# FNet mixing with a gated SwiGLU on one core: a written issue order for gate/up, and the later stages' preparation in three pieces

## The chip, the core and the metric

The kernel runs on one core of a Trainium2 chip. A core has a matrix engine (PE, with PEld as its weight loads), a vector engine (DVE), a scalar engine (ACT), a general engine (POOL, which here mostly issues DMAs) and a sync engine (SP, which here only issues DMAs). Each engine takes its own instructions in the order of its program and waits, at the head of that order, until what the instruction needs is there. The metric is device time in microseconds (us) of one execution; before the change it was 740.35 us (median of three runs, 739.05 to 740.51).

## What is computed

```python
def reference(A_x, A_dft_seq_re, A_dft_seq_im, A_dft_hid_re, A_dft_hid_im,
              B_x, B_w1, B_w3, B_w2, gate_w):
    x = A_x                                             # 1 x 2048 x 512, float32
    g = sigmoid((x * gate_w).sum(-1, keepdims=True))
    a = einsum("bsd,ed->bse", x, A_dft_hid_re)
    b = einsum("bsd,ed->bse", x, A_dft_hid_im)
    y = einsum("ts,bse->bte", A_dft_seq_re, a) - einsum("ts,bse->bte", A_dft_seq_im, b)
    h = silu(einsum("bsd,df->bsf", x, B_w1)) * einsum("bsd,df->bsf", x, B_w3)   # f = 1376
    out = einsum("bsf,fd->bsd", h, B_w2)
    return g * y + (1 - g) * out
```

## The kernel before

**Arithmetic.** Every float32 operand of a matrix product is split into a rounded high part and the remaining low part (`split`, lines 109 to 111: ACT copies the high part out, DVE subtracts it from the source to get the low part). A product is three matmuls: high by high, high by low, low by high (`mm3`, line 113). On top of that, 2x2 block products are done with seven block products in place of eight, from sums and differences of the blocks ("forms").

**Stages.** The first stage is gate/up: 22 items, each one pair of gate and up weight blocks (`c`, 128 columns of `w1` and of `w3`) with one half of the tokens (`g`). Items 0 to 8 are `c` 0 to 8 with `g` 0, items 9 to 12 are `c` 9 and 10 with both halves, items 13 to 21 are `c` 0 to 8 with `g` 1. Item 0 is done plainly; the others go through `gate_up(n)` in a loop over `n`. After them come the main stages: steps (`step(m)`) of 12 matmuls that multiply the sequence DFT blocks (`cc`), then the stored results of gate/up (`hsp`), then intermediate results (`zsp`) with stationary forms of `x`, `w2` and the hidden DFT.

**An item.** It has seven products of six matmuls each. Two of them, "first" products, belong to item `n + 3` (`first1`, `first2`, LOOK = 3), five to item `n`. In PE's order: product 4 of item `n` into bank X (from `wb`), product 5 into bank Z (`wb`), first product of item `n + 3` (`wa`), product 3 into X (`wb`), product 2 into Z (`wa`), the second product of item `n + 3` into bank Y (`wa`), and product 6 into X (`wb`). Between them ACT and DVE read the banks: u2 copies X (line 292), u4 copies Z (line 294), s1 copies the first product (line 249), `u4 += X` (line 297), `u2 += Z` (line 299), `u2 *= s1` (line 300), `s1 += Y` (line 257) and its silu (line 259), the silu of X (line 304) and `g1 *= u4` (line 305). POOL then stores h (line 283). A product that adds into a bank must wait for the copy that reads it first: product 3 for u2, product 2 for u4, product 6 for `u4 += X`. The bank of the first product of item `n + 3` is the one that the silu of line 304 of item `n - 1` reads last.

**Weights.** `wa` (three forms) is split from the loaded `ws`; `wb` (four forms) needs four DVE sums of 256 columns (lines 224 to 227) and a split. `wb` of `c` 0 to 8 is stored (line 232) and loaded back (line 209) for the second half of the tokens.

**Work for later stages** is woven into the items through a dictionary `extra`, run at the end of an item: the second half of `x` for gate/up (`xo_sum`, `split_xo`, items 3 to 9), four blocks of `w2` (`prep_w2`, items 9 to 12, stored to `w2sp` by POOL at lines 450 and 452) and seven of the eight stationary forms of `x` (`make_a`, items 13 to 19). A block is loaded at the end of the item before. `w2` works in four wide tiles (`wide`, pool f4_a) and two tiles for the parts (`parts`, pool zo_a); each `prep_w2` takes both of the latter, so that the next one's ACT copies wait for the stores of the last.

**Order.** In the loop over the items only PE's and SP's orders are as written (`manual_schedule` with these two engines, line 566); those of ACT, DVE and POOL are laid out by the framework's planner from its own estimates when the program is built. From line 575 on all engines go as written. After the loop the pools of gate/up are closed and their memory is given to those of the main stages: the buffers of `cc` blocks from 4 on lie over `wb` and `wa`, the tiles of `load_a2` (line 592) over the second half of `x`.

Of the kernel before, what the change touches and what calls it, by code (L numbers as in the profile page):

```python
# [26 lines left out]
K = 9  # L27
XO_AT = 3
W2_AT = (9, 10, 11, 12)
A1_AT = (13, 14, 15, 16, 17, 18, 19)  # L30


@with_exitstack
def fnet_swiglu_gate_kernel(
# [63 lines left out]
    def wide(name):  # L98
        return take(F4, [P, 1024], F32, name)
# [4 lines left out]
    def free(*tiles):  # L104
        for t in tiles:
            _, places, at = HELD.pop(id(t))
            places.append(at)

    def split(hi, lo, src):
        nc.scalar.activation(hi, src, AF.Copy)  # L110
        nc.vector.tensor_sub(lo, src, hi.bitcast(F32))  # L111

# [31 lines left out]
    def splits1(m, t1):  # L144
        split(flat(t1[:, 0, 1:4]), flat(t1[:, 1, 1:4]), m[:, :768])

    def forms1(r, m, t1):
        sums1(r, m, t1)
        splits1(m, t1)

# [24 lines left out]
    def flat_x(ap):  # L175
        return ap.rearrange("p q n -> p (q n)")
# [11 lines left out]
    def sum_xo(g, k, t):  # L188
        ST[g, k] = t
        nc.vector.tensor_sub(t, *(ST[g, v] for v in SUMS[k]))  # L190

    def split_xo(g, k):
        o = XO[g][:, :, OPS.index(k)]
        split(flat_x(o[:, 0]), flat_x(o[:, 1]), ST[g, k])

    WS, WA, WB = {}, {}, {}

    def back(w):
        return w >= NC and SETS[w] > 0
# [7 lines left out]
    def load_wb(w):  # L207
        WB[w] = wbp.tile([P, 2, 4, 256], F32R, tag="wb", name=f"wb{w}")
        nc.sync.dma_start(WB[w].bitcast(F32), wbsp[SETS[w]])

    def prep_wa(w, lo=0, hi=3):

        if lo == 0:
            WA[w] = wap.tile([P, 2, 3, 256], F32R, tag="wa", name=f"wa{w}")
        t = WA[w]
        split(t[:, 0, lo:hi].rearrange("p a n -> p (a n)"),
              t[:, 1, lo:hi].rearrange("p a n -> p (a n)"),
              WS[w][:, lo:hi].rearrange("p a n -> p (a n)"))

    def prep_wb(w):  # L220

        r = WS.pop(w)
        u = wup.tile([P, 4, 256], F32, tag="wu", name=f"wu{w}")
# [3 lines left out]
        nc.vector.tensor_sub(u[:, 3], r[:, 1], u[:, 1])  # L227
        t = WB[w] = wbp.tile([P, 2, 4, 256], F32R, tag="wb", name=f"wb{w}")
        split(t[:, 0].rearrange("p a n -> p (a n)"), t[:, 1].rearrange("p a n -> p (a n)"),
              u.rearrange("p a n -> p (a n)"))  # L230
        if w < K:
            nc.gpsimd.dma_start(wbsp[w], t.bitcast(F32))

# [29 lines left out]
    def put_score(n, j, gate):  # L263


        c, g = ITEMS[n]
        if c < NC - 1:
            return
        if j == 0:
            SC[g] = wide(f"sc{g}")  # L270
        t = SC[g].rearrange("p (b n) -> p b n", b=2)
        nc.scalar.activation(t[F % P :, j], gate[F % P :], AF.Copy)
        if j == 1:
            nc.gpsimd.dma_start(gs[2 * g : 2 * g + 2].rearrange("b o n -> o b n"),
                                t[F % P : F % P + 1])
            extra.setdefault(n + 1, []).append(lambda: free(SC[g]))

# [6 lines left out]

    def second(n, between):
# [6 lines left out]
        nc.scalar.activation(u2, x, AF.Copy)  # L292
# [6 lines left out]
        nc.vector.tensor_add(u2, u2, z)  # L299
        nc.vector.tensor_mul(u2, s1, u2)  # L300
        between[1]()
        prod(x, n, 6, 2, False, True)
        put_score(n, 1, x)
        nc.scalar.activation(g1, x, AF.Silu)  # L304
        nc.vector.tensor_mul(g1, g1, u4)
        store_h(n, h)

    extra = {}

    def gate_up(n):  # L310
        last = NI - 1

        def b0():
            w = WSET[min(n + LOOK, last)] + 1
            if w < len(SETS) and w not in WA and w not in WS:
                load_w(w, 0, 3 if back(w) else 4)
            if n < last and WSET[n + 1] not in WB:
                prep_wb(WSET[n + 1])
            if n + LOOK <= last:
                first1(n + LOOK)  # L320

        def b1():
            if n + LOOK < last and WSET[n + LOOK + 1] not in WA:
                prep_wa(WSET[n + LOOK + 1])
            if n + LOOK <= last:
                first2(n + LOOK)

        if n < last and WSET[n + 1] not in WB and back(WSET[n + 1]):
            load_wb(WSET[n + 1])
        if n + LOOK <= last and WSET[n + LOOK] not in WA:  # L330
            prep_wa(WSET[n + LOOK])
        second(n, (b0, b1))
        for f in extra.get(n, ()):
            f()

# [90 lines left out]
    WS.pop(0)  # L426
    load_w(4)


    def xo_sum(k, b):  # L430
        return lambda: (sum_xo(1, k, ST[1, b]), split_xo(1, k))

    extra[XO_AT - 2] = [lambda k=k: load_xo(1, k) for k in ("B11", "B21", "B12", "B22")]
    for n, f in enumerate((lambda: split_xo(1, "B11"), lambda: split_xo(1, "B21"),
                           xo_sum("T1", "B11"), xo_sum("T2", "B11"), xo_sum("T3", "B12"),
                           xo_sum("T4", "B21"), lambda: split_xo(1, "B22"))):
        extra[XO_AT + n] = [f]
    for n, k in enumerate((("B12",), ("B11", "B21"), ("B22",))):
        extra[XO_AT + 4 + n].append(lambda k=k: free(*(ST[1, b] for b in k)))

    W2R = {}

    def load_w2(p):
        W2R[p] = wide(f"w2r{p}")
        nc.sync.dma_start(W2R[p], w2[p])

    def prep_w2(p):
        r, m, t1, t2 = W2R.pop(p), wide(f"w2m{p}"), parts(f"w2a{p}"), parts(f"w2b{p}")
        forms1(r, m, t1)
        nc.gpsimd.dma_start(w2sp[0][p], t1.bitcast(F32))  # L450
        forms2(r, t2[:, :, :3])
        nc.gpsimd.dma_start(w2sp[1][p], t2[:, :, :3].bitcast(F32))
        free(r, m, t1, t2)

# [5 lines left out]

    def make_a(p, pl=None):
        A1.append((pl or a1).tile([P, 2, 4, 256], F32R, tag=f"a1_{p}", name=f"a1_{p}"))
        r, m = XR.pop(p), wide(f"xm{p}")
        forms1(r, m, A1[p])
        free(r, m)

    for p, n in enumerate(W2_AT):
        extra.setdefault(n - 1, []).append(lambda p=p: load_w2(p))
        extra.setdefault(n, []).append(lambda p=p: prep_w2(p))
    for p, n in enumerate(A1_AT):  # L470
        extra.setdefault(n - 1, []).append(lambda p=p: load_a(p))
        extra.setdefault(n, []).insert(0, lambda p=p: make_a(p))
    extra.setdefault(NI - 2, []).append(lambda: load_a(NG - 1))
    extra[NI - 1] = [lambda: load_c(2)]

# [101 lines left out]
    split_c(1)  # L577
    close(*gate_pools)
# [6 lines left out]
    ZO[:0] = [(zo_b, f"zo_{k}") for k in range(2, 4)]  # L585
    make_a(NG - 1, a1b)
    advance(-1)
# [110 lines left out]
    def step(m):  # L698
# [17 lines left out]
        ni = cols(blk, q, form) // 512  # L716
        for r in range(2):
            sl = slice(r * P, (r + 1) * P)
            for n, zn in steps:
                for i in range(ni):  # L720
                    w = ws[2 * n + i]
                    b = slice(i * 512, (i + 1) * 512)
                    mm3(ps[r], w[:, 0, FORM[k], sl], w[:, 1, FORM[k], sl], zn[:, 0, b], zn[:, 1, b],
                        own and n == 0 and i == 0, n == NQ[blk] - 1 and i == ni - 1, not own)
# [136 lines left out]
```

## Time and profile before

| What | Value |
|---|---|
| Median of three runs | 740.35 us (739.05 to 740.51) |
| The profiled execution, its own time | 739.09 us |
| Its span, first to last instruction | 737.2 us |
| Granted PE clock, mean over the span | 0.998 |
| Matmuls | 3089 |
| DVE busy | 575.8 us (78%) |
| ACT busy | 366.2 us (50%) |
| DMA | 186.16 MB, mean 253 GB/s |

All times below are from the span's start. A row of the timeline gives the start, the length, the engine, the line, the operation, the tiles written and read, and how many instructions were merged (x6); in square brackets stands how long the engine had been idle before it and what released it. Matmuls overlap, so the step from the start of one row to the start of the next tells how long a product occupies PE, not the row's length.

### The profile page before, as it was taken

The numbers are of one execution on the slowest core, as the hardware profiler recorded it, in microseconds if no ns is written. First come the engines' busy times: TensorE is split into PE (matmuls) and PEld (weight loads), VectorE is DVE, ScalarE is ACT, GpSimd is POOL, SyncE is SP. The second block draws the span as 40 slices with busy tenths as digits, with TensorE's granted clock in tenths as the row PEclk, the third lists the DMA queues.
The fourth block names the chain that finished last, engine by engine and source line by source line (L and its number), as shares of the span: only waits on it lengthen the run. The fifth ranks groups of instructions, "written<-read, shape, count | busy, mean of one in ns | idle before, by whom it ended". The sixth has DMA issues, their size and how long they took to land.

```text
span 737.2 us, 8514 instructions
## 1 busy us (share of the span) xinstructions
PE 714.3 (97%) x3089; PEld 578.1 (78%) x3089; DVE 575.8 (78%) x717; ACT 366.2 (50%) x485; POOL 50.6 (7%) x74
## 2 busy tenths in 40 slices
PE   9999998899999899999999999999999999999997
PEld 6788876688887687888888887887778888887786
DVE  6999885757656887887798759985878596693996
ACT  6775553555433664445454445354535445444361
POOL 0111111110000010001000010001001001000000
PEclk9999999999999999999999999999999999999999
DMA  6665676667769757775967495829999689698862
GB/s 256 231 262 221 261 273 221 247 207 265 266 226 368 286 145 217 280 269 178 271 230 269 140 284 196 338 71 264 353 418 401 149 324 316 162 370 267 282 220 98
DMA packets 49625, 186.16 MB, mean 253 GB/s; under 512 B 5168, under 2 KB 5296, under 8 KB 44976
## 3 DMA queue, kind: packets, MB, share of 16 engines
q1 hardware_dynamic: 39728, 143.15, 53.6%
q0 software_dynamic: 9568, 41.96, 18.8%
q8 instruction: 24, 0.39, 0.2%
q10 hardware_dynamic: 288, 0.52, 0.2%
q14 instruction: 17, 0.14, 0.1%
HBM read 128.45 MB, written 57.16 MB: 252 GB/s over the span
## 4 chain that ended last, share of the span: by engine, by line
PE 45%; DMA 20%; issue 14%; DVE 13%; ACT 6%; SPq 1%; POOL 0%; ACTq 0%; POOLq 0%; DVEq 0%
PE P L115 24%; PE X L115 11%; DMA B<-cc 8%; PE Z L115 5%; DVE zo L111 5%; PE Y L115 3%; ACT zo L110 3%; DMA B<-zsp 3%; DMA B<-hsp 2%; DMA w2sp<-w2b 2%; DVE B L535 2%; DMA xs<-xn 1%; DMA dsp<-late 1%; PE C L115 1%; DMA p5g<-gs 1%
## 5 line engine op out<-in xcount | busy, mean ns | idle before, releaser
L115 PE MATMUL P<-zo,a 128*128 128x512 f32 x1344 | 311.4, 392 | 8.1 <-DVE zo L111 6.1
L115 PEld LDWEIGHTS P<-zo,a 128*128 128x128 f32 x1344 | 252.4, 189 | 66.9 <-DVE zo L111 10.9
L110 ACT ACTIVATE zo<-B 128x1024 fp32r<-128x1024 f32 (+1 forms) x182 | 187.6, 1044 | 214.9 <-DVE B L535 67.4
L111 DVE TENSOR_TENSOR zo<-B,zo 128x1024 fp32r<-128x1024 f32 (+1 forms) x182 | 216.9, 1204 | 88.5 <-ACT zo L110 87.7
L115 PE MATMUL P<-zo,H 128*128 128x512 f32 x468 | 106.5, 389 | 0.2 <-DVE zo L111 0.2
L115 PEld LDWEIGHTS P<-zo,H 128*128 128x128 f32 x468 | 87.8, 188 | 18.8 <-DVE zo L111 0.6
L115 PE MATMUL X<-xo,wb 128*128 128x512 f32 x378 | 93.6, 391 | 3.9 <-ACT h L292 3.9
L535 DVE TENSOR_TENSOR B<-B,B 128x1024 f32<-128x1024 f32 (+1 forms) x78 | 92.9, 1191 | 2.2 <-DMA B<-hsp 2.0
L115 PEld LDWEIGHTS X<-xo,wb 128*128 128x128 f32 x378 | 70.3, 188 | 21.2 <-ACT h L292 6.3
L115 PE MATMUL P<-zo,Y 128*128 128x512 f32 x336 | 77.5, 391 | 1.1 <-DVE zo L111 0.8
L115 PEld LDWEIGHTS P<-zo,Y 128*128 128x128 f32 x336 | 62.8, 188 | 15.6 <-DVE zo L111 2.7
L115 PE MATMUL X<-xo,wa 128*128 128x512 f32 x126 | 32.9, 392 | 4.3 <-ACT h L304 3.5
L115 PE MATMUL Y<-xo,wa 128*128 128x512 f32 x126 | 32.1, 389 | 0.0
L115 PE MATMUL Z<-xo,wb 128*128 128x512 f32 x126 | 32.1, 389 | 0.0
L115 PE MATMUL Z<-xo,wa 128*128 128x512 f32 x126 | 32.0, 389 | 0.0
L115 PEld LDWEIGHTS X<-xo,wa 128*128 128x128 f32 x126 | 23.4, 188 | 10.4 <-ACT h L304 4.4
L115 PEld LDWEIGHTS Z<-xo,wa 128*128 128x128 f32 x126 | 23.7, 188 | 5.0
L115 PEld LDWEIGHTS Z<-xo,wb 128*128 128x128 f32 x126 | 23.6, 188 | 4.9
L115 PEld LDWEIGHTS Y<-xo,wa 128*128 128x128 f32 x126 | 23.6, 188 | 4.9
L297 DVE TENSOR_TENSOR u<-u,X 128x512 f32<-128x512 f32 x21 | 14.4, 685 | 16.6 <-PE X L115 16.5
L551 POOL DMA_DIRECT2D B<-cc x16 | 13.7, 857 | 197.5 <-DVE zo L111 182.8
L110 ACT ACTIVATE wa<-ws 128x768 fp32r<-128x768 f32 (+2 forms) x21 | 17.0, 811 | 20.0 <-PE Z L115 11.7
(107 smaller groups left out, 530.8 us busy)
## 6 DMA issues: line engine op xcount, KB each, us to landing
B<-cc SPq DMA_DIRECT2D x64, 512.0 KB, 6.7
hsp<-h POOLq DMA_DIRECT2D x22, 512.0 KB, 5.2
B<-hsp SPq DMA_DIRECT2D x20, 512.0 KB, 9.6
wbsp<-wb POOLq DMA_DIRECT2D x8, 1024.0 KB, 5.1
wb<-wbsp SPq DMA_DIRECT2D x8, 1024.0 KB, 5.1
B<-cc POOLq DMA_DIRECT2D x16, 512.0 KB, 10.6
B<-zsp SPq DMA_DIRECT2D x16, 512.0 KB, 7.4
H<-w2sp SPq DMA_DIRECT2D x6, 1024.0 KB, 10.6
```

The costliest lines, as they stand in the source:

```text
L110: nc.scalar.activation(hi, src, AF.Copy)
L111: nc.vector.tensor_sub(lo, src, hi.bitcast(F32))
L115: nc.tensor.matmul(ps, u, v, start=first and n == 0, stop=last and n == 2, skip_group_check=chain)
L297: nc.vector.tensor_add(u4, u4, x)
L535: nc.vector.tensor_add(t, t, RAW[blk, b, q][:, :n])
L551: nc.gpsimd.dma_start(src, block(blk, "B12", q), accum_op=ALU.add)
```

## The change

All engines now go as written from item 1 on (one `manual_schedule` before the loop). `gate_up` writes the whole item out. The preparation for later stages is cut in three: sums, high part (ACT), low part (DVE, with the stores and the freeing of tiles). The sums run in `early` (after u2's copy), the high parts in `mid` (after product 3), the low parts in `early` of the next item; loads and frees run in `at_end`. `w2` blocks go to items 9, 11, 13 and 15 in place of 9 to 12, forms of `x` to items 12, 14 and 16 to 20 in place of 13 to 19. Forms of `x` are summed in place (`sums1_here`), without a tile of their own for the sums and with one split of 1024 columns in place of one of 256 and one of 768; the order of the forms differs for it (`FORMS`). The two score rows share one wide tile. The loads of the first `cc` blocks and their splits go into the last items.

```diff
-XO_AT = 3
-W2_AT = (9, 10, 11, 12)
-A1_AT = (13, 14, 15, 16, 17, 18, 19)
+W2_AT = (9, 11, 13, 15)
+A1_AT = (12, 14, 16, 17, 18, 19, 20)
...
+    def sums1_here(r):
+
+        a21, a11, a12, a22 = (r[:, i * 256 : (i + 1) * 256] for i in range(4))
+        nc.vector.tensor_sub(a22, a22, a21)
+        for d, v, w in ((a21, a22, a11), (a12, a12, a21)):
+            nc.vector.scalar_tensor_tensor(d, v, -1.0, w, op0=ALU.mult, op1=ALU.subtract)
...
+        nw = WSET[n + 1] if n < last else 0
+        if nw in WB or nw == 0:
+            nw = None
+        elif back(nw):
+            load_wb(nw)
+            nw = None
+        wa = WSET[n + LOOK + 1] if n + LOOK < last else 0
+        if wa in WA or wa == 0:
+            wa = None
+        else:
+            load_w(wa, 0, 3 if back(wa) else 4)
+
         prod(x, n, 4, 4, False, True)
         nc.scalar.activation(u2, x, AF.Copy)
+        run(early, n)
         prod(z, n, 5, 5, True, True)
         nc.scalar.activation(u4, z, AF.Copy)
-        between[0]()
+        if nw is not None:
+            sums_wb(nw)
+        if n + LOOK <= last:
+            first1(n + LOOK)
+        if nw is not None:
+            high_wb(nw)
         prod(x, n, 3, 3, False, True)
         nc.vector.tensor_add(u4, u4, x)
+        if nw is not None:
+            low_wb(nw)
+        run(mid, n)
         prod(z, n, 2, 6, False, True)
         nc.vector.tensor_add(u2, u2, z)
         nc.vector.tensor_mul(u2, s1, u2)
-        between[1]()
+        if wa is not None:
+            WA[wa] = wap.tile([P, 2, 3, 256], F32R, tag="wa", name=f"wa{wa}")
+            parts_a = wa_parts(wa, 0, 3)
+            high(parts_a[0], parts_a[2])
+        if n + LOOK <= last:
+            first2(n + LOOK)
+        if wa is not None:
+            low(*parts_a)
         prod(x, n, 6, 2, False, True)
         put_score(n, 1, x)
         nc.scalar.activation(g1, x, AF.Silu)
         nc.vector.tensor_mul(g1, g1, u4)
         store_h(n, h)
...
+        run(at_end, n)
...
+    for n, (k, b) in enumerate((("B11", ""), ("B21", ""), ("T1", "B11"), ("T2", "B11"),
+                                ("T3", "B12"), ("T4", "B21"), ("B22", ""))):
+        if b:
+            do(early, n + 2, lambda k=k, b=b: sum_xo(1, k, ST[1, b]))
+        do(mid, n + 2, lambda k=k: high(*xo_parts(1, k)[::2]))
+        do(early, n + 3, lambda k=k: low(*xo_parts(1, k)))
...
+    def sums_w2(p):
+        W2R[p] += [wide(f"w2m{p}"), parts(f"w2a{p}"), parts(f"w2b{p}")]
+        r, m, t1, t2 = W2R[p]
+        sums1(r, m, t1)
+        nc.vector.tensor_sub(r[:, :256], r[:, 256:512], r[:, :256])
+
+    def high_w2(p):
+        for v in w2_parts(p):
+            high(*v[::2])
+
+    def low_w2(p):
+        a, b, c = w2_parts(p)
+        low(*a)
+        nc.gpsimd.dma_start(w2sp[0][p], W2R[p][2].bitcast(F32))
+        low(*b)
+        low(*c)
+        nc.gpsimd.dma_start(w2sp[1][p], W2R[p][3][:, :, :3].bitcast(F32))
+        free(*W2R.pop(p))
...
+    for n in range(NI):
+        if n in W2_AT:
+            p = W2_AT.index(n)
+            do(at_end, n - 1, load_w2, p)
+            do(early, n, sums_w2, p)
+            do(mid, n, high_w2, p)
+            do(early, n + 1, low_w2, p)
+        if n in A1_AT:
+            p = A1_AT.index(n)
+            do(at_end, n - 1, load_a, p)
+            do(early, n, lambda p=p: sums1_here(XR[p]))
+            do(mid, n, high_a, p)
+            do(early, n + 1, low_a, p)
+    do(at_end, NI - 3, lambda: load_c(0))
+    do(at_end, NI - 2, load_a, NG - 1)
+    do(at_end, NI - 2, lambda: load_c(1))
+    do(early, NI - 1, lambda: sums1_here(XR[NG - 1]))
+    do(mid, NI - 1, lambda: split_c(0))
+    do(at_end, NI - 1, lambda: split_c(1))
...
+    FORMS = {"F": FORM | {"P1": 1, "P5": 3, "P6": 0, "P3": 2}, "H": FORM, "Y": FORM}
...
-    order = tc.manual_schedule(engines={mybir.EngineType.PE, mybir.EngineType.SP})
-    order.__enter__()
+    ctx.enter_context(tc.manual_schedule())
     for n in range(1, NI):
         gate_up(n)
-        if ITEMS[n] == (NC - 1, 1):
+        if ITEMS[n] == (NC - 1, 0):
             close(xo0_cm)
             a1_cm, a1 = pool("a1", 1, "left")
-
-    order.__exit__(None, None, None)
-    ctx.enter_context(tc.manual_schedule())
-    split_c(0)
-    split_c(1)
     close(*gate_pools)
...
-    make_a(NG - 1, a1b)
+    high_a(NG - 1)
+    low_a(NG - 1)
     advance(-1)
```

More of the change, by code (lines that the diff above doesn't have):

```diff
@@ L209, in load_wb, with wa_parts @@
         nc.sync.dma_start(WB[w].bitcast(F32), wbsp[SETS[w]])
+    def wa_parts(w, lo, hi):
+        return (*(flat(WA[w][:, h, lo:hi]) for h in range(2)), flat(WS[w][:, lo:hi]))
     def prep_wa(w, lo=0, hi=3):
@@ L283, in store_h, with run, gate_up @@
         nc.gpsimd.dma_start(o.rearrange("b p n -> p b n"), h.rearrange("p (b n) -> p b n", b=2))
-    def second(n, between):
+    early, mid, at_end = {}, {}, {}
+    def run(work, n):
+        for f in work.get(n, ()):
+            f()
+    def gate_up(n):
+        last = NI - 1
         x, s1 = G.pop(n)
@@ L306, in second @@
         store_h(n, h)
[L308 to L334, printed above, removed]
+        run(at_end, n)
     load_w(0, 0, 1)
@@ L427, in fnet_swiglu_gate_kernel @@
     load_w(4)
[L430 to L439, printed above, removed]
+    prep_wa(4)
@@ L441, in fnet_swiglu_gate_kernel @@
+    for n, k in ((7, "B12"), (7, "B11"), (8, "B21"), (9, "B22")):
+        do(early, n, lambda k=k: free(ST[1, k]))
     W2R = {}
     def load_w2(p):
[L444 to L453, printed above, removed]
+        W2R[p] = [wide(f"w2r{p}")]
+        nc.sync.dma_start(W2R[p][0], w2[p])
@@ L459, in load_a, with parts_a1, high_a, low_a @@
         nc.sync.dma_start(XR[p], xn[p])
[L461 to L474, printed above, removed]
+    def parts_a1(p):
+        return flat(A1[p][:, 0]), flat(A1[p][:, 1]), XR[p]
+    def high_a(p):
+        A1.append((a1b if p == NG - 1 else a1).tile([P, 2, 4, 256], F32R, tag=f"a1_{p}",
+                                                    name=f"a1_{p}"))
+        high(*parts_a1(p)[::2])
+    def low_a(p):
+        low(*parts_a1(p))
+        free(XR.pop(p))
+    for n in range(NI):
[17 more added lines that the diff above has]
+    do(at_end, NI - 1, lambda: split_c(1))
     CHAIN = (("P1", "B11"), ("P5", "T1"), ("P6", "T2"), ("P3", "B22"),
@@ L716, in step @@
         ni = cols(blk, q, form) // 512
+        f = FORMS[kind][k]
         for r in range(2):
```

70 lines of the change are left out of this document (45 added, 25 removed).

## The prediction

> **What bounds the kernel now.** I read the page's first block, then the busy time by stretches of 20 us, then PE's timeline where a stretch is not full.
>
> ```profile
> span 737.2 us, 8514 instructions
> PE 714.3 (97%) x3089; PEld 578.1 (78%) x3089; DVE 575.8 (78%) x717; ACT 366.2 (50%) x485; POOL 50.6 (7%) x74
> ```
>
> ```profile
> 40.00:60.00 20.00, 20.00 (x90) 16.45 (x89) 20.00 (x31) 12.93 (x20) 2.58 (x5) 1.00 0.61 238
> 100.00:120.00 20.00, 16.29 (x71) 12.77 (x69) 14.00 (x28) 8.64 (x16) 1.98 (x3) 1.00 0.62 236
> 120.00:140.00 20.00, 18.00 (x75) 13.93 (x76) 14.09 (x23) 10.40 (x20) 3.91 (x6) 1.00 0.68 241
> 140.00:160.00 20.00, 18.34 (x81) 14.83 (x81) 10.15 (x16) 9.47 (x16) 2.53 (x4) 1.00 0.61 218
> 160.00:180.00 20.00, 20.00 (x90) 16.57 (x89) 14.01 (x25) 10.20 (x17) 1.46 (x2) 1.00 0.73 251
> 240.00:260.00 20.00, 17.80 (x69) 13.38 (x67) 18.20 (x23) 13.09 (x18) 1.13 (x2) 0.91 0.70 260
> ```
>
> The columns after the length are busy time and count of PE, PEld, DVE, ACT and POOL, then PE's clock, DMA share and GB/s. PE bounds the kernel, so an edit is worth what it takes from PE's idle time. At 40 to 60 PE is full although DVE is full too, at 160 to 180 it is full with room on all others; in gate/up it loses time at 100 to 160, where neither DVE nor ACT is near full. That is waiting, not work.
>
> ```profile
> 106.26 1.57 PE L115 MATMUL X<-xo,wa 128*128 128x512 f32 x6
> 109.51 1.65 PE L115 MATMUL X<-xo,wb 128*128 128x512 f32 x6 [1.68 <-ACT h L292]
> 120.39 1.65 PE L115 MATMUL X<-xo,wa 128*128 128x512 f32 x6 [2.43 <-ACT h L304]
> 131.84 1.66 PE L115 MATMUL X<-xo,wa 128*128 128x512 f32 x6 [1.09 <-ACT h L304]
> 145.28 1.65 PE L115 MATMUL X<-xo,wb 128*128 128x512 f32 x6 [1.66 <-ACT h L292]
> 149.51 2.88 PE L115 MATMUL X<-xo,wb 128*128 128x512 f32 x12
> 152.23 1.52 PE L115 MATMUL Z<-xo,wb 128*128 128x512 f32 x6
> ```
>
> ```profile
> 114.11 0.42 ACT L110 ACTIVATE w2a<-w2r 128x256 fp32r<-128x256 f32 x1 [3.69 <-DMA w2r<-w]
> 118.44 0.63 ACT L110 ACTIVATE w2b<-w2r 128x512 fp32r<-128x512 f32 x1 [3.91 <-DMA w2sp<-w2b]
> 119.74 0.60 ACT L304 ACTIVATE h<-X 128x512 f32<-128x512 f32 x1
> ```
>
> From 149.51 to 152.23 twelve matmuls take 2.72 us: 0.227 each, 1.36 a product, 9.52 an item. PE waits for ACT copies and silus of lines 292 and 304, which are not late for their own inputs: ACT stands in its order at a `w2` copy, first for the load of `w2r`, then 3.91 us for the store of the previous `w2` block, which must leave the parts tile; the silu that frees PE's bank runs behind it at 119.74. From the row at 106.26 to that at 149.51 there are 25 products, 34.0 us, in 43.25: 9.25 us lost.
>
> The second loss is at the end of gate/up:
>
> ```profile
> 223.26 1.52 PE L115 MATMUL Z<-xo,wb 128*128 128x512 f32 x6
> 225.94 0.50 PE L115 MATMUL P<-zo,a 128*128 128x512 f32 x1 [1.16 <-ACT zo L110]
> 231.32 4.92 PE L115 MATMUL P<-zo,a 128*128 128x512 f32 x21
> 231.51 0.96 SPq L592 DMA_DIRECT2D xs<-xn  x2
> 240.72 0.43 DVE L154 TENSOR_TENSOR xs<-xs 128x256 f32<-128x256 f32 x1 [1.72 <-DMA xs<-xn]
> 244.67 7.34 PE L115 MATMUL P<-zo,a 128*128 128x512 f32 x24 [1.57 <-DVE zo L111]
> ```
>
> ```profile
> SPq L592 <- PE X L115: 0.2, 1, 0.2
> ```
>
> Four matmuls of the main stage (P) were put between the last item's products, the first behind a 1.16 us wait. From 223.26 four products would end at 228.70; the item ends at T = 231.32, 2.62 later. What follows hangs on T: the `xs` loads need the memory of the half of `x` that the last product reads (the wait of L592 for PE X), are issued at T + 0.2, and the first form made from them starts at T + 9.4. Behind that, in DVE's order, stands the split that step 4 needs, and PE goes on at 244.67, T + 13.35.
>
> **The change, part by part.** *`w2` in three pieces, every second item.* High parts no longer follow the sums at once, and a parts tile is asked for again two items later. The block loaded at the end of item n - 1 is summed after 1.36 us of item n, as before, but the load's wide tile was freed an item earlier, so that SP can issue it early in n - 1. The store goes out early in n + 1 and ACT asks for the tile in n + 2, some 8.7 us later (worked out under the slower rival). The stores land in:
>
> ```profile
> wb<-wbsp SPq DMA_DIRECT2D x8, 1024.0 KB, 5.1
> hsp<-h POOLq DMA_DIRECT2D x22, 512.0 KB, 5.2
> w2sp<-w2a POOLq DMA_DIRECT2D x4, 1024.0 KB, 5.6
> xr<-xn SPq DMA_DIRECT2D x8, 512.0 KB, 7.7
> ws<-w SPq DMA_DIRECT2D x9, 384.0 KB, 6.4
> w2sp<-w2b POOLq DMA_DIRECT2D x4, 768.0 KB, 7.4
> ```
>
> 5.6 us for the tile that is needed first. So ACT no longer stands there: minus 9.25.
>
> *The order through an item.* The strict order can make a chain of its own, through DVE and ACT from one item's `g1 *= u4` to the next: low part and sum of the other half of `x`, four `wb` sums, high and low part of `wb`, two operations on u2, `s1 += Y`, two silus, `g1 *= u4`.
>
> ```profile
> L300 DVE TENSOR_TENSOR h<-s,h 128x512 f32<-128x512 f32 x21 | 14.4, 688 | 0.3
> L111 DVE TENSOR_TENSOR wb<-wu,wb 128x1024 fp32r<-128x1024 f32 x11 | 13.4, 1219 | 1.9 <-ACT wb L110 1.9
> L259 ACT ACTIVATE s<-s 128x512 f32<-128x512 f32 x21 | 13.2, 627 | 8.9 <-DVE s L257 8.7
> L110 ACT ACTIVATE wb<-wu 128x1024 fp32r<-128x1024 f32 x11 | 11.6, 1055 | 1.0 <-DVE wu L227 1.0
> L227 DVE TENSOR_TENSOR wu<-ws,wu 128x256 f32<-128x256 f32 x11 | 4.6, 420 | 0.1
> 44.28 0.68 DVE L299 TENSOR_TENSOR h<-h,Z 128x512 f32<-128x512 f32 x1
> 44.88 0.95 DVE L111 TENSOR_TENSOR wa<-ws,wa 128x768 fp32r<-128x768 f32 x1
> ```
>
> Three operations of 1024 columns on DVE (3.66), four of 256 (1.68), four of 512 (2.75), one ACT copy (1.06) and two silus (1.25) are 10.4 us. Neighbours overlap, though (44.28 to 44.88 is 0.60 for an operation of 0.68), which takes some 0.08 from nine links: 9.6. Against an item's 9.52 the lag grows by 0.1 to 0.9 us in items 4 to 7, which alone hold both pieces of `x`; without them the chain is 7.4 to 8. The tightest cover is `u4 += X`: the last item's `g1 *= u4` ends 1.5 us into the item, low part and sum take it to 3.9, the `wb` sums to 5.6, product 3 is there at 5.6, so it ends at 6.3; product 6 needs it at 8.16. Of a lag of 0.4 to 3.6 us 1.8 is covered: 0 to 1.8 us lost; I take 0.3, by the overlapping rows. In the last three items, of five products, product 6 comes at 5.44 and `u4 += X` ends at about 5.0: 0 to 1.0, taken 0.2. Before item 1 the order is the planner's as before, but what it merges with differs; I bound that by one wait like that at 131.84, 1.1 us, on both sides, and take 0.
>
> *DMA in items 14 to 17.* By the rows above item 14 now moves `wb`, `ws`, one `w2r`, h and both `w2` stores, 4224 KB or 4.33 MB, and item 15 2.49 MB; 16 and 17 the same. That is 13.64 MB in 38.1 us.
>
> ```profile
> 218.00:228.00 10.00, 8.84 (x38) 6.77 (x38) 4.14 (x6) 4.36 (x7) 0.73 (x1) 1.00 0.99 382
> 228.00:238.00 10.00, 9.46 (x42) 7.54 (x41) 8.53 (x13) 3.45 (x5) 0.72 (x1) 1.00 0.99 339
> ```
>
> At a share of 0.99 the engines moved 339 to 382 GB/s: 35.7 to 40.2 us, 0 to 2.1 too long. On POOL the h store now stands behind the `w2` stores of its item; u2 of the item after next waits for it. Taken 0.4. The parts tile asked for in item 15 sits behind this traffic: 0 to 2.0, taken 0.4.
>
> *Forms of `x` in place.* One DVE operation of 1220 ns for one of 768 and one of 256 columns (950 and 420): 0.15 less on DVE for each of seven blocks, in a stage where DVE has 6 us in 20 free. Nothing; at most 1.0 if DVE were late there. The shared score tile and the order of the forms add no instruction.
>
> *The end of gate/up.* PE's order no longer mixes P into the last item: minus 2.62, and its four matmuls (0.9 us) come after T, inside the wait before step 4. On SP the first `cc` load moves ahead of the last `wb` reload and the second behind it; the third and fourth now lie over `wb` and go when item 20 has ended, still 6.8 us before T. Steps 0 to 3 take T to T + 10.9, so step 4 still waits. SP issues four `cc` loads just before T that it issued 1.9 us before T; I let `xs` land 0 to 1.0 later, taken 0.5.
>
> **The sum.** 9.25 + 2.62 = 11.9 us off; 0.3 + 0.2 + 0.4 + 0.4 + 0.5 = 1.8 on. Span 737.2 - 10.1 = 727.1. The profiled execution's own time, 739.09, is 1.9 above its span: 729.0. The median of the runs is 1.3 above that execution: 730.2.
>
> **One rule weighed.** The 24 matmuls from 244.67 last 7.34 us where 24 times 0.227 and the last one's tail make 5.6: 1.7 us at a lower clock (0.91 in that stretch), after 1.57 us of idling. After 2.43 us at 120.39 the clock stayed 1.00. The Trainium skill, page "TensorE: Matmul & The Clock Gate", section "Part 1: The HAM clock gate", has the clock halved after an idle window of about 3.4 us; neither wait here is that long, so the trace agrees at 120.39 and not at 244.67.
>
> **The rivals.** (1) *The clock stays up.* PE's short waits after T merge into one of 2.2 to 2.7 us before step 4. At 120.39 such a wait did not lower the clock; at 244.67 a string of shorter ones did. Without the slow stretch: 728.5. By that rule of the Trainium skill this is the case that comes. (2) *The bounds are met.* Chain, DMA and parts tile cost 1.8 + 2.1 + 2.0 in place of 1.1: 735.0. For it: chain and traffic are within a few per cent of what fits; against it: items 8 and later have slack to take up a lag. (3) *The stall only moves.* ACT again stands at `w2` or `xr` for as long as now, at other items: the 9.25 come back, 739.5. For it: `xr` takes 7.7 us to land; against it: each load and store has most of an item more. (4) *Slower: ACT behind the stores, three times.* The `w2` store of item n + 1 goes out about 3.0 us in (0.2 for the last matmul's tail, by which the row at 149.51 outlasts its 2.72, silu 0.6, product 0.7, low part 0.95, POOL 0.6); ACT comes to the same tile 9.52 + 1.36 + 0.2 + 0.6 = 11.7 us in, 8.7 later. Behind it stand a copy of 0.42 and u4's of 0.6, which product 2 needs at 14.96: the store may land up to 10.9 us after issue. Beyond that each us stops PE in items 11, 13 and 15. It undoes the gain from 10.9 + 10.1 / 3 = 14.3 us on; at 16 us it costs 15.3, so 745.1. For it: POOL's transfers share the engines with 2 MB of loads an item, and `w2b` takes 7.4. Against it: items 10 and 12 carry no `wb` reload.
>
> **Chances.** Forecast 0.52, (1) 0.14, (2) 0.18, (3) 0.05, (4) 0.11. The likeliest time is 730. Its own range is 727 to 733; to hold 8 in 10 I go from 725.5 (the clock stays up, all additions at 0 and the start of gate/up better by 1.1) to 738.5 (rival 2 with a lost us at the start and some traffic more). About 0.2%, 1.5 us, is what a measurement of this kernel can tell from no change. Faster: 0.52 + 0.14 + 0.18 = 0.84. Same: 0.05, the moved stall. Slower: 0.11.
>
> **What would show it.** ACT's waits for `w2sp` and `w2r` gone; PE full from item 2 to item 21, with products 1.36 apart; T near 220; no P between X and Z; the `xs` wait still ending near T + 9.4 and step 4 starting near T + 13.8. PE waits on line 297's result in items 5 to 8 would show the chain; a late h store or `wb` in items 14 to 17 the traffic. The prediction is wrong if PE stands in gate/up for more than 4 us in sum after item 1, or if the main stages take up what gate/up gives.

## The result, and the profile after

| What | Before | After |
|---|---|---|
| Median | 739.79 us (739.05 to 740.51, four runs) | 730.37 us (729.59 to 733.1, four runs) |
| Ratio of the times | 1 | 0.9879 [0.9851, 0.9908] |
| The profiled execution, its own time | 739.09 us | 730.07 us |
| Its span | 737.2 us | 727.9 us |

The change saves 9.4 us by the medians and 9.3 in the profiled spans. The first block of the changed kernel's page and its busy time by stretches (PE, PEld, DVE, ACT, POOL, then PE's clock, DMA share, GB/s):

```profile
span 727.9 us, 8512 instructions
PE 711.7 (98%) x3089; PEld 578.2 (79%) x3089; DVE 579.1 (80%) x709; ACT 366.1 (50%) x477; POOL 50.7 (7%) x74
```

```profile
56.00:94.00 38.00, 38.00 (x169) 31.44 (x168) 33.38 (x49) 21.22 (x31) 4.75 (x8) 1.00 0.56 212
100.00:120.00 20.00, 20.00 (x90) 16.51 (x89) 15.81 (x27) 13.13 (x21) 2.71 (x4) 1.00 0.41 137
120.00:140.00 20.00, 20.00 (x90) 16.57 (x89) 15.58 (x29) 10.55 (x19) 3.22 (x5) 1.00 0.53 199
140.00:160.00 20.00, 19.42 (x86) 15.74 (x86) 16.51 (x27) 12.60 (x20) 3.26 (x5) 1.00 0.88 307
200.00:220.00 20.00, 18.89 (x84) 15.29 (x83) 14.13 (x23) 8.09 (x12) 2.19 (x3) 1.00 0.93 319
220.00:240.00 20.00, 17.14 (x69) 13.10 (x67) 14.52 (x18) 10.50 (x13) 1.63 (x3) 0.94 0.99 363
152.10:190.20 38.10, 38.10 (x170) 31.55 (x169) 28.20 (x46) 18.61 (x30) 5.42 (x8) 1.00 0.94 354
```

The work is the same: 3089 matmuls, DVE's and ACT's busy times within 3.3 us. From 100 to 140, where PE had 16.29 and 18.00 of 20 us, it has all 40, and from 152.1 to 190.2, items 14 to 17, all of 38.10 us (the last row). Between 56 us and step 4, PE's waits of 0.5 us and more are in three places, read from its timeline:

```profile
145.09 1.65 PE L120 MATMUL X<-xo,wa 128*128 128x512 f32 x6 [0.58 <-ACT h L367]
207.82 1.52 PE L120 MATMUL Z<-xo,wb 128*128 128x512 f32 x6
210.45 1.66 PE L120 MATMUL X<-xo,wb 128*128 128x512 f32 x6 [1.11 <-ACT h L339]
220.14 1.52 PE L120 MATMUL X<-xo,wb 128*128 128x512 f32 x6
221.50 11.31 PE L120 MATMUL P<-zo,a 128*128 128x512 f32 x48
234.08 0.49 PE L120 MATMUL P<-zo,a 128*128 128x512 f32 x1 [1.28 <-ACT zo L109]
236.16 4.44 PE L120 MATMUL P<-zo,a 128*128 128x512 f32 x12 [1.58 <-DVE zo L112]
```

No P stands between the last item's products any more, and T, where uninterrupted P begins, is 221.50 instead of 231.32: 9.82 us earlier. Step 4 resumes at 236.16, T + 14.66 (before T + 13.35), so 8.51 us of it remain there. The other 0.8 of the span lies behind that. From there to the end the ten profiles here that leave the main stages alone take 490.5 to 492.7 us, so 0.8 is within what that stretch varies by itself.

The waits behind the 1.11 at 210.45 and behind step 4, from the timelines of ACT, POOL, SP and DVE:

```profile
201.63 0.72 POOL L309 DMA_DIRECT2D hsp<-h  x1 [7.14 <-DVE h L368]
209.80 0.60 ACT L339 ACTIVATE h<-X 128x512 f32<-128x512 f32 x1 [2.54 <-DMA hsp<-h]
222.20 0.92 SPq L664 DMA_DIRECT2D xs<-xn  x2
232.21 0.42 DVE L162 TENSOR_TENSOR xs<-xs 128x256 f32<-128x256 f32 x1 [3.17 <-DMA xs<-xn]
234.88 1.22 DVE L112 TENSOR_TENSOR zo<-B,zo 128x1024 fp32r<-128x1024 f32 x1
```

The copy of u2 (line 339) needs one of two h buffers, and stands there for a store issued at 201.63; it starts 8.2 us after that. The DMA issues from 200 to 206 (count, KB each, median us to landing) show what the store had beside it:

```profile
wb<-wbsp SPq DMA_DIRECT2D x1, 1024.0 KB, 5.3
xr<-xn SPq DMA_DIRECT2D x1, 512.0 KB, 6.1
B<-cc SPq DMA_DIRECT2D x1, 512.0 KB, 8.4
hsp<-h POOLq DMA_DIRECT2D x1, 512.0 KB, 8.1
```

These are the items with five products, 6.8 us each: the store is longer than the item. Before step 4 the picture is the old one: DVE waits for `xs` until T + 10.7, and the split of `zo` that PE wants ends behind it.

### The profile page after: what moved, and what is told of

The parts are those of the page before. It is cut to its first block, busy times and chain, and to the rows that moved or that the text cites. A ratio compares the mean times of both kernels' runs of the same rounds, so it can differ in the third digit from the quotient of the medians.

```text
span 727.9 us, 8512 instructions
## 1 busy us (share of the span) xinstructions
PE 711.7 (98%) x3089; PEld 578.2 (79%) x3089; DVE 579.1 (80%) x709; ACT 366.1 (50%) x477; POOL 50.7 (7%) x74
## 4 chain that ended last, share of the span: by engine, by line
PE 43%; DMA 20%; issue 17%; DVE 12%; ACT 4%; SPq 1%; POOL 1%; POOLq 0%; ACTq 0%; DVEq 0%
PE P L120 21%; PE X L120 12%; DMA B<-cc 7%; PE Z L120 6%; DMA B<-hsp 5%; DVE zo L112 5%; PE Y L120 3%; ACT zo L109 3%; DMA p5g<-gs 3%; DMA B<-zsp 2%; DVE B L612 2%; PE C L120 2%; DMA dsp<-late 1%; DMA hsp<-h 1%; DVE zp L827 1%
## 5 line engine op out<-in xcount | busy, mean ns | idle before, releaser
L309 POOL DMA_DIRECT2D hsp<-h x22 | 16.2, 735 | 134.6 <-DVE h L368 115.1
L284 ACT ACTIVATE s<-s 128x512 f32<-128x512 f32 x21 | 13.2, 631 | 24.4 <-DVE s L282 24.3
## 6 DMA issues: line engine op xcount, KB each, us to landing
H<-w2sp SPq DMA_DIRECT2D x6, 1024.0 KB, 10.6
```

The lines of the kernel that those rows point to most:

```text
L284: nc.scalar.activation(s1, s1, AF.Silu)
L309: nc.gpsimd.dma_start(o.rearrange("b p n -> p b n"), h.rearrange("p (b n) -> p b n", b=2))
```

## The experiments

Every kernel was compared with the kernel before on the same chip, whose median was 739.93, 739.79 and 739.26 us in the three groups of runs. The first four take the change apart into its order, its spacing of the `w2` blocks and its pieces; the others change the kernel after.

**The order alone**, in the kernel before.

```diff
-    order = tc.manual_schedule(engines={mybir.EngineType.PE, mybir.EngineType.SP})
+    order = tc.manual_schedule()
```

> The kernel before, with ACT, DVE and POOL also going as written from item 1 on; w2 and x forms still in one piece at the end of an item, w2 in items 9 to 12. Theory (pieces and spacing matter, the order alone does not bring the gain): ACT's u2 copy now stands behind a whole preparation; a w2 block needs some 4 us of alternating ACT and DVE work (ACT 0.42, DVE 1.26, ACT 0.84, ACT 1.05), so u2 of the next item ends about 5.5 us in where product 3 comes at 4.08: 1.5 to 2.5 us lost in each of four items and 0 to 0.5 in the seven with x forms, 6 to 13 us in place of the 9.25 between 106 and 150 us; the 2.6 us at the end of the stage come off. 733 to 741 us. Rival (the written order alone brings it, the planner's order was the fault): 729 to 732 us.

792.46 us (790.77 to 793.3), ratio 1.07 [1.0678, 1.0722]. It is 52.5 us slower, outside both ranges: the theory had 733 to 741, the rival a gain. Only the theory's first half holds, that the order alone does not bring the gain. PE's waits from 60 to 292 (total, times, longest) put most of it on the copy of u2 and the silu:

```profile
PE X L115 <- ACT h L292: 29.5, 15, 5.0
PE X L115 <- ACT h L304: 10.6, 4, 3.8
```

The silu (line 304) is late because ACT's copy of `wa`, which stands ahead of it, waits for its load:

```profile
ACT wa L110 <- DMA ws<-w: 32.0, 4, 10.6
```

From 60 to 292 ACT waits for no `w2` store. What holds it up at line 292 is seen in the fourth kernel.

**The spacing alone**, in the kernel before.

```diff
-W2_AT = (9, 10, 11, 12)
+W2_AT = (9, 11, 13, 15)
```

> The kernel before with w2 blocks in items 9, 11, 13 and 15 in place of 9 to 12, nothing else; ACT, DVE and POOL as the planner lays them out. Theory (ACT stood behind the store of the block before): the waits for w2sp go, the waits for freshly loaded w2r and xr stay where the planner puts them; of 9.25 us lost 3 to 6 come back: 733 to 737 us. Rival (the planner's order is the fault, whatever the spacing): 738.5 to 741 us, with the waits at other items.

741.51 us (738.42 to 743.01, ten runs), ratio 1.0014 [0.9996, 1.0032]: no change, and half a us above the rival's range. ACT's timeline of this kernel shows why spacing gave nothing:

```profile
115.08 0.42 ACT L110 ACTIVATE w2a<-w2r 128x256 fp32r<-128x256 f32 x1 [4.51 <-DMA w2r<-w]
120.09 0.63 ACT L110 ACTIVATE w2b<-w2r 128x512 fp32r<-128x512 f32 x1 [4.59 <-DMA w2sp<-w2b]
```

The waits are those of before (3.69 and 3.91), and no shorter. The planner still puts `w2` copies where their inputs have not landed, and the silu behind them.

**No spacing**, in the kernel after: its order and pieces, `w2` in four items running. (The form of item 12 moves to 13 to make room.)

```diff
-W2_AT = (9, 11, 13, 15)
-A1_AT = (12, 14, 16, 17, 18, 19, 20)
+W2_AT = (9, 10, 11, 12)
+A1_AT = (13, 14, 16, 17, 18, 19, 20)
```

> The changed kernel with w2 blocks again in four items in a row, 9 to 12 (x forms then from 13), everything else as changed. Theory (a parts tile must have an item and more for its store): ACT asks for the tile 2.2 us into the item in which the store is issued at about 3.0 after the low part, so the DVE low part comes first but ACT waits 6 to 7 us for the landing, u4's copy ends at 10 to 11 us where product 2 needs it at 5.4: 4 to 6 us lost in each of items 10, 11 and 12, 742 to 748 us, slower than the kernel before. Rival (three pieces in a written order are enough): 729 to 733 us.

755.94 us (755.39 to 759.48), ratio 1.0225 [1.0192, 1.0257]: slower, as the theory has it, and by more than its 742 to 748. The first `w2` tile is stored early in item n + 1, and ACT asks for it again in that same item. First POOL's issue of the store, then ACT's next use of the tile, then PE:

```profile
116.83 0.57 POOL L507 DMA_DIRECT2D w2sp<-w2a  x1 [0.39 <-issue]
124.59 0.42 ACT L109 ACTIVATE w2a<-w2r 128x256 fp32r<-128x256 f32 x1 [9.28 <-DMA w2sp<-w2a]
125.55 2.93 PE L120 MATMUL Z<-xo,wa 128*128 128x512 f32 x6 [6.78 <-ACT u L342]
```

This happens three times: PE waits 20.3 us in all for the u4 copy (line 342) that stands behind the `w2a` copy, up to 7.9 at once where 4 to 6 were expected. Each wait also leaves the clock low: the six matmuls take 2.93 us where 1.66 is the rule. This is the stall of rival 4, at a spacing of one item.

**Order and spacing without the pieces**, in the kernel before: both edits of the first two experiments.

> The kernel before with all engines as written and w2 in items 9, 11, 13 and 15: order and spacing as in the change, but each preparation still in one piece at the end of an item. Theory (the pieces are what a written order needs: u2's copy stands behind the whole preparation): the waits for u2 stay 0.8 to 1.8 us in items with pieces of x and 3 to 5 us, with a slow clock behind them, in the four w2 items; 770 to 790 us against 792 without the spacing. Rival (the spacing mends the written order, the 52 us were the stores): under 760 us.

776.44 us (776.16 to 778.03), ratio 1.0513 [1.0482, 1.0543]: within the theory's range. From 60 to 292 ACT waits neither for a `w2` store nor for `ws`, and the 10.6 us of the silu in the order alone are gone; they are the larger part of the 16.0 us between the two kernels. ACT's timeline at one `w2` block, and PE behind it:

```profile
127.94 0.41 ACT L110 ACTIVATE w2a<-w2r 128x256 fp32r<-128x256 f32 x1
130.92 0.84 ACT L110 ACTIVATE w2a<-w2m 128x768 fp32r<-128x768 f32 x1 [2.58 <-DVE w2m L142]
133.12 0.42 ACT L110 ACTIVATE w2b<-w2r 128x256 fp32r<-128x256 f32 x1 [0.84 <-DVE w2r L154]
133.45 0.58 ACT L292 ACTIVATE h<-X 128x512 f32<-128x512 f32 x1
134.08 2.93 PE L115 MATMUL X<-xo,wb 128*128 128x512 f32 x6 [4.97 <-ACT h L292]
```

A whole preparation, sums and splits by turns on DVE and ACT, is written between an item's last silu and the next item's u2 copy. For 5.5 us (127.94 to 133.45) the copy that frees PE's bank has to stand behind it. At all `w2`, `x` and form items together, by PE's waits from 60 to 292 (total, times, longest), this is most of what the kernel loses:

```profile
PE X L115 <- ACT h L292: 32.5, 13, 6.2
```

The four kernels and the two ends give a table (medians):

| ACT, DVE, POOL order | `w2` spaced | Pieces | us |
|---|---|---|---|
| planner | no | no | 739.9 |
| planner | yes | no | 741.5 |
| written | no | no | 792.5 |
| written | yes | no | 776.4 |
| written | no | yes | 755.9 |
| written | yes | yes | 730.4 |

No row but the last is under 739. With the written order, the pieces (and the smaller edits that come with them) are worth 46.0 us, 776.4 to 730.4, and the spacing 25.5, 755.9 to 730.4. The pieces under the planner's order were not tried.

**Low parts in the item of the high parts** (two pieces instead of three), in the kernel after.

```diff
-        do(early, n + 3, lambda k=k: low(*xo_parts(1, k)))
+        do(mid, n + 2, lambda k=k: low(*xo_parts(1, k)))
...
-            do(early, n + 1, low_w2, p)
+            do(mid, n, low_w2, p)
...
-            do(early, n + 1, low_a, p)
+            do(mid, n, low_a, p)
```

> The changed kernel with the low parts right behind the high parts in mid of the same item, so two pieces in one item in place of three over two. Theory (it is the room for the stores and the place in the item that count, not the third piece): DVE does the same work, waits at most 1 to 2 us an item for ACT's high part, covered in most items: 729.5 to 733 us. Rival (the pieces over two items keep PE full): 'u2 += Z' comes late in items 2 to 20, u2's and the silus' chain passes 9.52 us, 1 us and more lost in each of some fifteen items: over 740 us.

734.16 us (732.45 to 736.01), ratio 0.9926 [0.9898, 0.9954]: 3.8 us slower than the kernel after by the medians, a little above the theory's range and far from the rival's. No wait is large; PE's longest in gate/up after 100 us are 0.90 at 146.76 and 1.32 at 212.94. So with two pieces 42 of the 46 us are there, and the third is worth the last 3.8 or so: the runs of each of the two kernels spread over 3.5 us.

**Each form's split in two again**, in the kernel after.

```diff
+    def cut_a1(p):
+        return [(flat(A1[p][:, 0, i:j]), flat(A1[p][:, 1, i:j]), XR[p][:, i * 256 : j * 256])
+                for i, j in ((0, 1), (1, 4))]
...
-        high(*parts_a1(p)[::2])
+        for v in cut_a1(p):
+            high(*v[::2])
...
-        low(*parts_a1(p))
+        for v in cut_a1(p):
+            low(*v)
```

> The changed kernel with each x form made in gate/up split in two again (256 and 768 columns, ACT 0.42 and 0.84 for 1.06, DVE 0.42 and 0.95 for 1.22), the sums still in place. Theory (covered: neither DVE nor ACT is full there): no change, within 1 us of 730.4. Rival (the chain through an item is full): 0.15 to 0.4 us lost in each of eight items, 731.5 to 733.5 us.

731.07 us (730.14 to 733.05, five runs), ratio 0.9894 [0.9871, 0.9917], against 730.37 for the kernel after. PE's waits in gate/up stay as they were (0.57 us at 145.00, 1.1 at line 339). The extra splits cost 0.7 us by the medians, within the spread of the runs: the theory's. That DVE and ACT have room for them is the likely reason; it is not shown apart.

**The `xs` forms later**, in the kernel after. The forms from `xs` are put two steps further back in the order, and the gates four.

```diff
-        at(0, 2 * p + 1, make_a2, p)
-    at(0, 2, gates, 0)
+        at(0, 2 * p + 3, make_a2, p)
+    at(0, 6, gates, 0)
```

> The changed kernel with the second forms of x (which wait for the xs loads) two steps later in the first main block, and the gates of the first half at step 6 in place of 2; nothing left out. Theory (after gate/up the time hangs on T only because the xs wait stands ahead of step 4's split in DVE's order): the idle 1.28 and 1.58 us before step 4 go, and the slow clock behind them (1.7 us): 4 to 5 us less than the changed kernel, 725 to 727 us. Rival A (the cc loads themselves are late, the wait moves to a later step): 729 to 731. Rival B (the idle time goes, the slow clock comes anyway): about 727.5.

727.44 us (726.17 to 730.75), ratio 0.9832 [0.98, 0.9863]: 2.9 us better than after by the medians, 3.8 by the spans; its runs overlap those of after, but all runs of the two kernels below that hold this edit lie under them. PE's timeline, the stretch and SP's issue of the loads:

```profile
221.47 25.16 PE L120 MATMUL P<-zo,a 128*128 128x512 f32 x109
247.27 3.04 PE L120 MATMUL P<-zo,a 128*128 128x512 f32 x12 [0.64 <-DVE zo L112]
```

```profile
220.00:240.00 20.00, 20.00 (x89) 16.25 (x88) 19.58 (x22) 11.20 (x15) 0.72 (x1) 1.00 0.94 366
```

```profile
222.18 0.92 SPq L664 DMA_DIRECT2D xs<-xn  x2
```

T is the same (221.47), but 109 matmuls follow it without a gap, 25.16 us for 109 times 0.227 (24.7) and a tail. Neither the idle time nor the low clock of 0.94 before step 4 is left. The loads go out at the same time as in the kernel after (222.20); the split that PE needs no longer stands behind them. By the median this is rival B's 727.5, but its low clock is not in the trace, and the mean granted clock is 0.999 to 1.0 in three of the four runs (0.997 in the other), against 0.997 to 0.998 in those of the kernel after. Forms and gates were moved together; that the forms are what counts is read from DVE's wait of 3.17 us for `xs` ahead of the split, and was not tried apart.

**The first `cc` load an item later**, so that the h store has fewer loads beside it, in the kernel after.

```diff
-    do(at_end, NI - 3, lambda: load_c(0))
...
+    do(at_end, NI - 2, lambda: load_c(0))
```

> The changed kernel with the load of the first cc block at the end of item 20 in place of 19, nothing else. Theory (PE's 1.11 us before product 3 of item 20 is the u2 copy waiting for the h store of item 18, which stands behind that cc load on the DMA engines): the h store lands 1.3 us earlier (512 KB at about 390 GB/s), the wait at 210 us goes, T and the end come 1.0 to 1.3 us earlier. Rival (an item of five products is simply too short for two h buffers): the wait stays at 0.8 to 1.2 us and the time is the same.

730.07 us (729.69 to 730.86), ratio 0.9871 [0.9851, 0.9892]: the same, the rival's time. The store lands in 6.6 us instead of 8.1, as the theory has it, and the wait left 210.45, but it came back an item later. ACT and PE:

```profile
216.14 0.60 ACT L339 ACTIVATE h<-X 128x512 f32<-128x512 f32 x1 [2.30 <-DMA hsp<-h]
216.79 1.65 PE L120 MATMUL X<-xo,wb 128*128 128x512 f32 x6 [0.87 <-ACT h L339]
```

The traffic is moved, not removed: the next store is late in place of this one. T comes 0.5 us earlier (221.00), and step 4 no earlier (236.29).

**The first form of `x` in item 13**, so that item 12 holds less, in the kernel after. (The wide tile of the scores is freed first, for the load.)

```diff
-A1_AT = (12, 14, 16, 17, 18, 19, 20)
+A1_AT = (13, 14, 16, 17, 18, 19, 20)
...
-                at_end.setdefault(n + 1, []).append(lambda: free(SC[0]))
+                at_end.setdefault(n + 1, []).insert(0, lambda: free(SC[0]))
```

> The changed kernel with the first form of x in item 13 in place of 12 (the score tile is freed before the next load is placed). Theory (PE's 0.58 us at 145 us is the chain of DVE and ACT work through item 12, which holds w2 low parts, sums of an x form, wb sums and a score copy): without the x form's three sums of 0.42 the chain is 1.0 us shorter and the wait goes: 0.7 to 0.9 us less. Rival (it is the score copy on ACT, 0.6, that makes the silu late): 0.58 stays, no change.

729.81 us (729.54 to 730.48), ratio 0.9867 [0.9843, 0.9892], 0.6 us less than after by the medians, which the spread of the runs does not tell from nothing. The 0.58 at 145.09 is gone, as the theory has it, and 0.65 appears at the end of item 17, where ACT's silu (line 367) runs behind the copy of a late `wa`:

```profile
190.82 0.85 ACT L109 ACTIVATE wa<-ws 128x768 fp32r<-128x768 f32 x1 [5.27 <-DMA ws<-w]
192.72 1.66 PE L120 MATMUL X<-xo,wa 128*128 128x512 f32 x6 [0.65 <-ACT h L367]
```

In the kernel after the same copy waits too, and ends at nearly the same time:

```profile
190.77 0.85 ACT L109 ACTIVATE wa<-ws 128x768 fp32r<-128x768 f32 x1 [4.30 <-DMA ws<-w]
```

PE arrives earlier, the load does not: ACT waits 0.97 us longer for it and starts at the same time. What PE gains ahead of items 14 to 17 it hands back at their loads.

**These three together**, in the kernel after.

> The changed kernel with the three edits together: second forms of x and gates later, first cc load later, first form of x in item 13. If each wait is its own, the parts add: 730.4 - 3.0 - 1.2 - 0.8 = 725.4 us, span 722. Rival (a wait taken away before T comes back behind T, because the cc loads then are not there): 727 us.

727.28 us (726.23 to 728.42), ratio 0.9833 [0.981, 0.9855]. That is the rival's time, and that of the later `xs` forms alone; the parts do not add. In gate/up PE still waits 1.0 us once for line 339. T comes at 220.70, 0.77 earlier than with the later forms alone; where that is lost again behind T stays open.

**A third h buffer**, with the later `xs` forms: the h of item 19 goes into a parts tile that is idle by then.

```diff
-        h = hp.tile([P, 1024], F32, tag="h", name=f"h{n}")
+        spare = parts(f"h{n}") if n == NI - 3 else None
+        if spare is None:
+            h = hp.tile([P, 1024], F32, tag="h", name=f"h{n}")
+        else:
+            h = spare.rearrange("p h a n -> p (h a n)")[:, :1024].bitcast(F32)
...
+        if spare is not None:
+            free(spare)
```

> The changed kernel with the second forms of x and the gates later, as in the earlier run, and h of item 19 in a parts tile that is idle then, so that u2 of items 20 and 21 wait for stores that are one item older. Theory (the 1.1 us at 210, which moved to 217 when the cc load was put later, is an h buffer waiting for its store in items of 6.8 us): both waits go, the main stages start at 220.3 in place of 221.5, the time is 1 us below the 727.4 of that run. Rival (the DMA engines are full there and something else is late next, a wb or an x form): the wait turns up at another product and the start stays within 0.4 of 221.5.

725.99 us (725.28 to 727.55), ratio 0.9826 [0.98, 0.9851]: the fastest of all by its median, 4.4 us under the kernel after. The stretch in question, and T:

```profile
200.00:220.00 20.00, 20.00 (x90) 16.58 (x89) 15.66 (x25) 8.20 (x12) 2.19 (x3) 1.00 0.94 332
```

```profile
219.93 25.15 PE L120 MATMUL P<-zo,a 128*128 128x512 f32 x109
```

PE is full to T, which comes 1.54 us earlier than with two buffers (221.47), and the engines still move 332 GB/s at a share of 0.94. The h store issued at 201.50 still takes 8.1 us: a late store costs PE nothing once nobody asks for its buffer. How much of the 1.54 us reaches the end is open: against the later forms alone the median is 1.45 us lower, but the runs overlap, and the profiled spans are 724.3 and 724.1.

## Why the prediction held, step by step

**The 9.25 us at `w2`.** Right in mechanism and in size: from 100 to 150 one wait of 0.58 is left. Of ACT's waits for a DMA between 60 and 222 (total, times, longest) none is for `w2r`, and one of 0.7 us for `w2sp` (the last row):

```profile
ACT wa L109 <- DMA ws<-w: 9.7, 4, 4.3
ACT h L339 <- DMA hsp<-h: 3.6, 2, 2.5
ACT w2a L109 <- DMA w2sp<-w2a: 0.7, 1, 0.7
164.40 0.42 ACT L109 ACTIVATE w2a<-w2r 128x256 fp32r<-128x256 f32 x1 [0.70 <-DMA w2sp<-w2a]
```

That 0.7 says how close rival 4 was. The working had the store land after 5.6 us, ACT ask for the tile after 8.7, and PE stop from 10.9 on. In the changed kernel the stores and the weight loads issued from 105 to 200 land after:

```profile
w2sp<-w2a POOLq DMA_DIRECT2D x4, 1024.0 KB, 7.9
ws<-w SPq DMA_DIRECT2D x7, 384.0 KB, 7.2
```

So at the median the cover of 8.7 had 0.8 left. But the four `w2a` stores took 7.0, 7.0, 9.3 and 8.9 us, and the third, issued at 155.07, is the one that ACT waited for; only PE's margin, to 10.9, kept it from costing time. Before, stores and loads took 5.6 and 6.4 at the median. With the blocks in neighbouring items ACT waited 9.28 us and more. The spacing is needed, as the prediction had it. What it did not see is what the written order costs without the pieces: 37 us even where the blocks are spaced (739.3 to 776.4). It costed the order by its chain alone, and that with the pieces in place.

**The end of gate/up, 2.62.** Right in full: no P inside the last item. T was 219.45 by the two gains alone (231.32 less 9.25 and 2.62) and 220.75 with the additions ahead of it (0.3, 0.2, 0.4 and 0.4); it came at 221.50, and the two waits are nearly all of the 2.05 between 219.45 and that. By the starts of the products on both sides the wait of 0.58 cost 0.74 (142.99 plus 1.36, to 145.09) and that of 1.11 cost 1.27 (207.82 plus 1.36, to 210.45).

**The chain through DVE and ACT, taken 0.3.** The size was near, the place was not. The prediction looked to items 4 to 7, which hold both pieces of `x`; there (56 to 94) PE is full. It lost 0.58 in item 13 for the silu of item 12, which holds the low parts of a `w2` block, scores and a form of `x`, and moving the form away removed it.

**DMA in items 14 to 17, taken 0.4, and the parts tile, 0.4.** The engines moved 354 GB/s for 38.1 us, 13.5 MB where 13.64 was counted, at a share of 0.94; PE stood for none of it. So both terms were zero in place. But the traffic sets when `ws` arrives, and takes back what is won ahead of it.

**The short items, taken 0.2.** This term was mis-sized and put on the wrong instruction. The prediction had `u4 += X` as the late one; what was late was the u2 copy, behind an h store of some 8 us in items of 6.8, and it cost 1.11. The two h buffers had been named for items 14 to 17 only. It had priced that store at its median of 5.2 us, though in the kernel before one issued in the same stage, at 217.03, took 8.1. A third buffer took the wait away.

**The `xs` wait, taken 0.5.** Right that it stays, sized too small: the loads were issued 0.7 us after T instead of 0.2, and the first form came 1.3 us later after T than before (10.7 against 9.4). That it is the wait for `xs`, and not PE's work, which sets step 4 is shown by the later forms (moved together with the gates).

**The forms in place, taken nothing.** For the split confirmed to within 0.7 us; the sums in place were not undone by themselves.

**The rivals.** The clock did not stay up: PE's idle time became 1.28 and 1.58 us around one matmul, and the next twelve took 4.44 us, where twelve in gate/up take 2.88. The bounds of the chain and the traffic were not met, and the stall did not move as a whole; parts of rival 2 did come, in the places above.

**The sum.** The span came at 727.9 for 727.1. T was 0.75 later than the sum had it, step 4 a further 0.8, and the main stages gave some 0.8 back. The two gains had the size that they were given, the smaller terms did not: chain and short items cost 2.01 where 0.5 was taken, the two DMA terms nothing where 0.8 was taken, and the `xs` wait 1.3 where 0.5 was taken. That they came out so near is in part luck, and so is the median, 730.37 for 730.2: the profiled execution took 730.07 for 729.0, and the median lay 0.3 above it where 1.3 had been taken.

## What to carry to other kernels

A written order serves only if each instruction in it has its inputs by the time its engine gets there; a preparation that alternates between two engines has to be cut so that each piece finds the last one's result lying ready, or the written order costs more than the planner's, as it did here. Before a tile is reused, compare the time from its store's issue to the next use with the store's landing under the new traffic, not with a median over the old, and count every small ring of buffers (here two h tiles) against the shortest item it passes through. Where a late load cannot come earlier, look at what stands behind it in the order: moving that saved more here than moving the load's neighbours.

## What was not expected of the hardware

**The clock after a wait.** The long waits shown above were followed by a lower clock (the six matmuls behind 4.97 us took 2.93). For shorter ones the length did not decide. In the kernel with the spacing alone a single wait of 1.91 us was enough, whereas 2.43 us at 120.39 in the kernel before left the clock at 1.00:

```profile
193.94 2.23 PE L115 MATMUL X<-xo,wa 128*128 128x512 f32 x6 [1.91 <-ACT h L304]
192.00:202.00 10.00, 8.09 (x29) 6.49 (x29) 7.23 (x12) 5.37 (x10) 0.73 (x1) 0.83 0.59 235
```

The Trainium skill, page "TensorE: Matmul & The Clock Gate", section "Part 1: The HAM clock gate", halves the clock after an idle window of about 3.4 us; the trace agrees for the waits longer than that and not for this one, nor for those of 2.88 and 3.18 us in the order alone, behind which six matmuls took 2.93 and 2.92. What separates 1.91 from 2.43 stays open. Before step 4 the low clock cost 1.6 to 1.7 us in the kernels before and after, about as much as the wait of 1.58 itself; in the order alone the same wait, 1.56 us at 299.61, left the clock at 1.00.

**The price of a store.** The 512 KB h store took 5.2 us at the median before, and 8.1 at 201.63 in the kernel after, where 2 MB of loads were issued within the same 6 us. The same store, issued at 57.84, took 3.2. The stretches of the two flights, in columns as above (the last two are DMA share and GB/s):

```profile
57.84:61.04 3.20, 3.20 (x16) 2.65 (x15) 3.17 (x6) 1.20 (x2) 0.72 (x1) 1.00 0.43 164
201.63:209.73 8.10, 7.71 (x35) 6.04 (x33) 6.35 (x11) 2.44 (x4) 1.46 (x2) 1.00 0.99 368
```

So the time goes with the load on the DMA engines and not with the store's size. Of the h stores of the kernel after, the eight with a share of up to 0.57 over their flight took 3.1 to 3.2 us, and the eight with 0.98 and more 7.2 to 8.2. A median over both kinds is the time of neither.
